# Batch 3 of a fused attention and bilinear kernel: block sums on GpSimd, multiplications on VectorE, x sums earlier, unused products spread over Sinkhorn's rounds

## The chip, the cores and the metric

The kernel runs on one core of a Trainium2 chip. The metric is the device time of one execution in microseconds (us). Three runs of the kernel before took 234.43, 234.69 and 235.43 us; the median is 234.69 us. In the rows, PE is TensorE, PEld its weight loads, DVE VectorE, ACT ScalarE, POOL GpSimd and SP SyncE, which issues DMAs.

## The reference

Four batches of eight heads, 768 positions, head width 64. An 8x8 matrix per head is made nearly doubly stochastic by five rounds of Sinkhorn, it mixes the eight blocks of k and v, and each block of q attends to its mixed block. The result, 3072 rows of 512, goes through a bilinear feed-forward layer.

```
P = sort_net
for _ in range(5):
    P = exp(P - max(P));  P = P / sum(P, axis=-1);  P = P / sum(P, axis=-2)
k_sorted, v_sorted = P applied to the 8 blocks of k and v
attn = softmax(q_block @ k_sorted_block.T / 8)
x = (attn @ v_sorted_block), reshaped to 3072 x 512
out = ((x @ w_a) * (x @ w_b)) @ w_out        # 512 -> 1536 -> 512
```

## The kernel before

**Tiling.** The four batches follow each other. A batch has 768 rows, so x transposed (`xT`) is four tiles of 128 x 768 and the hidden layer (`hT`) twelve of them. In the feed-forward layer, a = x w_a and b = x w_b are made in pieces of 128 hidden units by 384 rows (four products of 128x128 with 384 columns each, line 372), ScalarE copies a from PSUM to SBUF, and VectorE multiplies it with b, which it reads from PSUM (line 404). While TensorE does the layer of one batch, `interleave` slips the next batch's attention units between the steps. The order of instructions on every engine is the order in which the program writes them.

**Block products with fewer multiplications.** The output product h w_out is done by `ffn_out_pair` in three units of seven block products (42 products on TensorE each) in place of eight. It needs sums of blocks of h: `h_sums(b, m, nm)` (line 460) makes, for the pair of hidden tiles m and m + 6, three instructions: `hs[0]` and `hs[1]` in one (768 elements per partition), `hs[2]` (384), and one that overwrites two blocks of h in place (768). All stand at line 475 and run on VectorE; with nm = 2 one instruction serves two pairs. They wait in the list `sums_due` and are let out by `some_sums` between other work, or all at once by `sums_for` ahead of the first output unit. That unit reads, in order: h as it is (two block products), `hs[1]` (`add1`), `hs[0]` (`add3`), `hs[2]` (`add2`), then the two overwritten blocks.

**Batch 3.** The last batch has no attention beside it, and its a is made in the same way from sums of blocks of x and of w_a. `x_sum(3, n)`, n = 0 to 4, makes the sums of x on VectorE (line 578); in the kernel before they run in the last two steps of batch 2, 0 and 1 after the third of the four parts of the last output unit, and 2, 3 and 4 after the fourth. Then `ab_four(b, m)`, for m = 0 to 5, handles one pair of hidden tiles with 30 products of 384 columns:

```
a_product(acc0); a_product(acc1); a_product(pf1)     # y = acc0 + acc1 + pf1
b(1,0); a_product(acc0); b(0,1) after a_product(acc1)  # middle blocks h(1,0), h(0,1)
a_product(acc0); a_product(acc1); b(0,0); b(1,1)     # corners: a = y - acc
```

The order on TensorE is acc0, acc1, pf1 (two products each), b(1,0) (four), acc0, acc1 (two each), b(0,1) (four), acc0, acc1 (two each), b(0,0), b(1,1) (four each). The two `acc` are PSUM tiles that take three block products each in turn, so TensorE may go on adding only when the earlier content was read. In the kernel before, ScalarE copies both acc to SBUF (lines 622, 624), GpSimd adds them to y (line 625), and VectorE adds pf1 (line 628). For the middle blocks ScalarE copies b and a to SBUF (lines 613, 618) and GpSimd multiplies (lines 632, 636). VectorE makes both corners (line 642) and multiplies them with b from PSUM (line 645). The h sums go to VectorE's list after m = 1, 3, 4 and 5, for the pairs 0 and 1, 2 and 3, 4, and 5.

**The start.** Sinkhorn's chain of small instructions on VectorE and ScalarE takes five rounds. Beside it TensorE runs products of zeros whose result nobody reads (`keep_busy`, line 181), and transposes q of batch 0 (`first_q`, line 202) when its DMA has landed. `pace(t, n)` is one such product that reads t, the row or column sums of a round, and so waits for them, followed by n more.

Of the kernel before, what the change touches and what calls it, by code (L numbers as in the profile page):

```python
# [9 lines left out]
FP32 = mybir.dt.float32  # L10
# [13 lines left out]
def kernel(  # L24
# [154 lines left out]
    def keep_busy(ps, n, cols=512):  # L179
        for _ in range(n):  # L180
            nc.tensor.matmul(ps[:, 0:cols], lhsT=warm[:, 0:P], rhs=warm[:, 0:cols],  # L181
                             start=True, stop=True)
# [15 lines left out]
    def first_q(hp):  # L198
        q_ps = psF.tile([P, NCH, P], BF16, tag="F", name="q_ps")
        for c in range(NCH):  # L200
            for e in range(2):
                nc.tensor.matmul(q_ps[e * D:(e + 1) * D, c, :],  # L202
                                 lhsT=q_first[:, 2 * hp + e, c * D:(c + 1) * D],
                                 rhs=ident, is_transpose=True)
        st["q_ps", hp] = q_ps
# [177 lines left out]
    def some_sums(n):  # L383
        for _ in range(min(n, len(sums_due))):
            sums_due.pop(0)[1]()
# [71 lines left out]
    def h_part(b, r, c, m):  # L457
        return hTs[b][:, c * KH + m, r * HW:(r + 1) * HW]

    def h_sums(b, m, nm):  # L460
        n0, n = (P, HW - P) if b == 0 else (0, HW)
        if b not in sums:
            sums[b] = ffp.tile([P, KH, 3, HW], BF16, tag="hs", name="hs")
        hT, hs = hTs[b], sums[b]

        def h(r, c, step):
            return _ap(hT, (c * KH + m) * S + r * HW + n0,
                       [[KO * S, P], [S, nm]] + [[step, 2]] * (step is not None) + [[1, n]])

        def s(i, k):  # L470
            return _ap(hs, (m * 3 + i) * HW + n0,
                       [[KH * 3 * HW, P], [3 * HW, nm]] + [[HW, k]] * (k > 1) + [[1, n]])

        turn = KH * S - HW
        return [("h", lambda to=to, x=x, y=y, op=op: nc.vector.tensor_tensor(  # L475
                    out=to, in0=x, in1=y, op=op))
                for to, x, y, op in (
                    (s(0, 2), h(0, 0, 0), h(0, 1, HW), ALU.add),
                    (s(2, 1), h(1, 0, None), h(1, 1, None), ALU.add),
                    (h(1, 0, turn), h(0, 0, KH * S + HW), h(1, 0, turn), ALU.subtract))]  # L480
# [72 lines left out]
    C11, C12, C21, C22 = (w_a_sb[:, r * 2:(r + 1) * 2, c * DFF // 2:(c + 1) * DFF // 2]  # L553
                          for r in range(2) for c in range(2))
    a_sums, x_sums = {}, {}
    spare = {}

    def a_sum(n, kc):
        x, y = (C11, C12, C21, C21, C11)[n], (C22, C22, C11, C22, C12)[n]
# [31 lines left out]

    def ab_four(b, m):
        hT = hT_of(b)
        if m < 2:
            spare[m] = ld.tile([P, 2, HW], FP32, tag="kv", name="two_a")
        s2 = spare[m % 2]
        acc = [psA.tile([P, 2, 512], FP32, tag="A", name="acc")[:, 0, 0:HW] for _ in range(2)]
        y = ld.tile([P, HW], FP32, tag="q2", name="y_a")

        def a_tile():  # L600
            return ffp.tile([P, HW], BF16, tag="a_sb", name="a_sb", bufs=4)

        def b_of(c, t):
            pf = psF.tile([P, 512], FP32, tag="F", name="pf")
            ab_mms(pf, w_b_sb, b, m + c * KH, t, range(KA))
            return pf[:, 0:HW]

        def h(c, t):
            return hT[:, m + c * KH, t * HW:(t + 1) * HW]

        def kept_b(c, t):
            b_sb = ld.tile([P, HW], FP32, tag="q2", name="b_sb")
            nc.scalar.copy(out=b_sb, in_=b_of(c, t))
            return b_sb

        def middle(n):
            a_sb = a_tile()
            nc.scalar.copy(out=a_sb, in_=acc[n])
            return a_sb

        a_product(acc[0], (b, 0, 0), a_sums[1], m)
        nc.scalar.copy(out=s2[:, 0], in_=acc[0])
        a_product(acc[1], (b, 1, 1), a_sums[2], m)
        nc.scalar.copy(out=s2[:, 1], in_=acc[1])  # L624
        nc.gpsimd.tensor_tensor(out=y, in0=s2[:, 0], in1=s2[:, 1], op=ALU.add)  # L625
        pf = psF.tile([P, 512], FP32, tag="F", name="pf1")[:, 0:HW]
        a_product(pf, 0, a_sums[0], m)
        nc.vector.tensor_tensor(out=y, in0=pf, in1=y, op=ALU.add)
        b_sb = kept_b(1, 0)
        a_product(acc[0], 1, C22, m, False)  # L630
        a_sb = middle(0)
        nc.gpsimd.tensor_tensor(out=h(1, 0), in0=a_sb, in1=b_sb, op=ALU.mult)
        a_product(acc[1], 2, C11, m, False)
        a_sb = middle(1)
        b_sb = kept_b(0, 1)
        nc.gpsimd.tensor_tensor(out=h(0, 1), in0=a_sb, in1=b_sb, op=ALU.mult)
        some_sums(1)
        corners = []
        for n in range(2):
            a_product(acc[n], 3 + n, a_sums[3 + n], m, False)  # L640
            a_sb = a_tile()
            nc.vector.tensor_tensor(out=a_sb, in0=y, in1=acc[n], op=ALU.subtract)
            corners.append(a_sb)
        for n in range(2):
            nc.vector.tensor_mul(out=h(n, n), in0=corners[n], in1=b_of(n, n))  # L645
            some_sums(1)
        if m in (1, 3, 4, 5):
            sums_due[:0] = h_sums(b, *((m - 1, 2) if m < 4 else (m, 1)))

# [54 lines left out]
    with tc.manual_schedule(engines={ET.PE, ET.Pool, ET.SP, ET.Activation, ET.DVE}):  # L706
        if True:
# [14 lines left out]
                copy(eng, p_rep[:, hf * NR:(hf + 1) * NR],  # L722
                     _ap(p_fin, hf * NR, [[NB * NB, BH], [1, NR], [0, CG // 2]]))

            keep_busy(heat[:, 0], 46, P)
            for hp in range(HP):
                first_q(hp)
                if hp % 2:
                    keep_busy(heat[:, 0], 34 if hp == 1 else 2, P)
            for it in range(5):  # L730
                rsum, csum = chain[0][it], chain[1][it]
                nc.scalar.activation(out=p_nat, in_=p_nat, func=AF.Exp)
                if it == 2:
                    with nc.allow_low_precision("sum of one one and zeros"):
                        nc.vector.reduce_sum(
                            out=mask, in_=_ap(ident, 0, [[P, P], [1, CG], [CG, NB]]),
                            axis=AX.X)
                nc.vector.reduce_sum(out=rsum, in_=p_nat, axis=AX.X)
                nc.vector.reciprocal(out=rsum, in_=rsum)
                if it == 4:  # L740
                    pace(rsum, 10)
                nc.vector.tensor_mul(out=p_nat, in0=p_nat,
                                     in1=_ap(rsum, 0, [[NB, BH], [1, NB], [0, NB]]))
                nc.vector.reduce_sum(out=csum, in_=p_nat.transpose([0, 2, 1]), axis=AX.X)
                nc.vector.reciprocal(out=csum, in_=csum)
                if it == 4:
                    pace(csum, 6)
                if it < 4:
                    nc.vector.tensor_mul(out=p_nat, in0=p_nat,
                                         in1=_ap(csum, 0, [[NB, BH], [0, NB], [1, NB]]))  # L750
                else:
                    nc.vector.tensor_mul(
                        out=p_fin.bitcast(BF16).rearrange("h (i j u) -> h i j u", i=NB, j=NB),
                        in0=_ap(p_nat, 0, [[NB * NB, BH], [NB, NB], [1, NB], [0, 2]]),
                        in1=_ap(csum, 0, [[NB, BH], [0, NB], [1, NB], [0, 2]]))
                if it == 3:
                    first_q_out(0, "act")
            first_q_out(1, "act")
            first_q_out(2, "act")
            replicate("dve", 0)  # L760
# [104 lines left out]
        for b in range(1, B):  # L865
            ab = {}

            def ab_begun(m, t, b=b, ab=ab):
                if b == 1 and m == t == 0:
                    for key in ((0, w_a_sb), (0, w_b_sb)):  # L870
                        pf = psF.tile([P, 512], FP32, tag="F", name="pf")
                        ab.setdefault(key[0], []).append(pf)
                        ab_mms(pf, key[1], b, 0, key[0], range(KA - 1))
                return ab.get(t, ()) if m == 0 else ()

            steps = [lambda m=m, t=t, b=b: ffn_ab(b, m, t, ab_begun(m, t))
                     for m in halves for t in range(2)]
            if b == B - 1:
                steps = [lambda m=m, b=b: ab_four(b, m) for m in range(KH)]
            steps += outs(b)  # L880
            if b == 2:
                steps[1] = after(steps[1], lambda: sums_due.extend(
                    a_sum(n, kc) for n in (2, 3, 0, 1, 4) for kc in range(2)))
                steps[-2] = after(steps[-2], lambda: (x_sum(3, 0), x_sum(3, 1)))
                steps[-1] = after(steps[-1], lambda: (x_sum(3, 2), x_sum(3, 3), x_sum(3, 4)))
            interleave(steps, units_full(b + 1) if b + 1 < B else [],
                       (1, 4, 8, 10, 13, 15, 17, 20, 21, 24, 25, 28))

# [29 lines left out]
```

## Time and profile before

| what | us |
|---|---|
| median of three runs (lowest to highest) | 234.69 (234.43 to 235.43) |
| the profiled execution, its own time | 233.79 |
| its span, first to last instruction | 232.0 |
| around the span (233.79 - 232.0) | 1.79 |
| busy: TensorE / VectorE / ScalarE / GpSimd | 225.8 / 158.4 / 120.9 / 87.7 |
| batch 3, products for a and b begin | 183.23 |
| batch 3, first output product | 214.12 |
| TensorE begins the last twelve products | 227.38 |
| granted TensorE clock, mean | 0.999 |

Times in rows are from the start of the span. A row of a timeline gives the start, the time from the first instruction's start to the last one's end, the engine, the line, the operation with its tiles and the count, and in brackets for how long the engine had idled and what released it. Rows of one engine overlap a little, since an instruction begins while the one before it drains: the distance between starts is what an instruction costs in a row of equals, and its duration what a follower waits.

### The profile page before, as it was taken

Reading aid. Unit: us, or ns where it says so; the run is one execution under the profiler, and the core shown is the slowest. Engines: PE = TensorE matmul, PEld = TensorE weight load, DVE = VectorE, ACT = ScalarE, POOL = GpSimd, SP = SyncE. Lnnn points to the kernel's source line nnn. Section 1 sums busy time; section 2 is a strip of 40 time slices with the busy share of each in tenths; the row PEclk is TensorE's granted clock in tenths of the full one; section 3 lists DMA queues with packets and bytes.
Section 4 is the critical chain, followed back from the end, with each engine's and each line's share of the span. In section 5 each row is a group of like instructions: output and inputs, shape, how many; then the busy total and the mean of one; then the engine's idle time right before and its main releaser. Section 6 shows DMA issues by size and latency. Waiting matters only on the chain.

```text
span 232.0 us, 5823 instructions
## 1 busy us (share of the span) xinstructions
PE 225.8 (97%) x2281; PEld 158.9 (68%) x2283; DVE 158.4 (68%) x352; ACT 120.9 (52%) x260; POOL 87.7 (38%) x116
## 2 busy tenths in 40 slices
PE   7999999999999999999999999999999989999994
PEld 7876766766549865666689865666698745555783
DVE  7776777446999334758886347778785675979732
ACT  3575854687633375655552375656543445544231
POOL 8779839840041555237622010000000156766000
PEclk9999999999999999999999999999999999999999
DMA  5999999999759999998999454224025300000042
GB/s 71 201 201 199 206 204 199 196 196 157 133 86 213 144 201 170 165 186 110 132 179 209 158 127 79 42 41 82 12 47 155 132 34 0 1 0 3 2 168 104
DMA packets 54859, 28.70 MB, mean 124 GB/s; under 512 B 33712, under 2 KB 51888, under 8 KB 54832
## 3 DMA queue, kind: packets, MB, share of 16 engines
q0 software_dynamic: 18832, 14.16, 44.8%
q1 hardware_dynamic: 35856, 14.04, 31.7%
q8 instruction: 18, 0.29, 0.5%
q10 hardware_dynamic: 144, 0.13, 0.2%
q14 instruction: 9, 0.07, 0.1%
HBM read 28.32 MB, written 6.29 MB: 149 GB/s over the span
## 4 chain that ended last, share of the span: by engine, by line
PE 86%; DVE 7%; issue 2%; DMA 2%; ACT 1%; POOL 0%; POOLq 0%; DVEq 0%
PE pf L372 44%; PE po L484 21%; PE mix L312 3%; PE o_ps L278 3%; PE acc L588 3%; DMA first<-in_q_dram 2%; PE sc L333 2%; PE heat L181 1%; DVE x_sum L578 1%; DVE hT L475 1%; PE mixh L224 1%; PE sc L237 1%; DVE hs L475 1%; PE xt_ps L269 1%; PE q_ps L202 1%
## 5 line engine op out<-in xcount | busy, mean ns | idle before, releaser
L372 PE MATMUL pf<-xT,w_b_sb 128*128 128x384 bf16 x384 | 77.9, 326 | 0.0
L404 DVE TENSOR_TENSOR hT<-a_sb,pf 128x384 bf16<-128x384 bf16 x72 | 39.7, 552 | 38.1 <-ACT a_sb L403 22.9
L372 PE MATMUL pf<-xT,w_a_sb 128*128 128x384 bf16 x280 | 57.5, 326 | 0.0
L372 PEld LDWEIGHTS <-w_b_sb 128*128 128x128 bf16 x384 | 37.5, 98 | 24.9
L403 ACT CAST a_sb<-pf 128x384 bf16<-128x384 f32 x70 | 34.0, 486 | 33.7 <-PE pf L372 28.7
L372 PEld LDWEIGHTS <-w_a_sb 128*128 128x128 bf16 x288 | 25.9, 98 | 14.3
L484 PE MATMUL po<-w_sum,hT 128*128 128x256 bf16 x264 | 31.9, 273 | 0.3 <-DVE hT L645 0.3
L625 POOL TENSOR_TENSOR y_a<-two_a 128x384 f32<-128x384 f32 x6 | 6.0, 1005 | 58.5 <-ACT two_a L624 58.5
L484 PEld LDWEIGHTS <-hT 128*128 128x128 bf16 x264 | 25.4, 98 | 3.9 <-DVE hT L645 0.7
L175 ACT CAST kv<-mix 128x384 bf16<-128x384 f32 x48 | 19.5, 493 | 4.7 <-PE mix L312 4.6
L338 ACT ACTIVATE eT<-sc 96x768 bf16<-96x768 f32 x24 | 18.1, 802 | 6.0 <-PE sc L333 6.0
L484 PEld LDWEIGHTS <-hs 128*128 128x128 bf16 x198 | 19.1, 98 | 2.5 <-DVE hs L475 0.4
L475 DVE TENSOR_TENSOR hs<-hT 128x768 bf16<-128x768 bf16 (+5 forms) x32 | 20.4, 652 | 0.4
L505 DVE TENSOR_TENSOR o<-y,po 128x256 f32<-128x256 f32 x22 | 9.2, 420 | 11.9 <-PE po L484 11.9
L498 ACT COPY s<-po 128x256 f32<-128x256 f32 x22 | 8.0, 374 | 17.8 <-PE po L484 17.8
L284 DVE TENSOR_TENSOR xp<-o_ps,rec 96x512 bf16<-96x512 f32 x24 | 16.5, 687 | 0.8
L484 PE MATMUL po<-w_out_sb,hs 128*128 128x256 bf16 x132 | 16.4, 273 | 0.0
L111 POOL COPY kvc<-kv 128x768 uint32<-128x768 uint32 x16 | 13.3, 843 | 7.5 <-PE mix L312 7.2
L498 ACT COPY o<-po 128x256 f32<-128x256 f32 x22 | 8.2, 372 | 15.0 <-PE po L484 15.0
L299 POOL COPY qc<-q 128x384 uint32<-128x384 uint32 x12 | 6.4, 535 | 23.3 <-DMA q<-in_q_dram 18.3
L100 POOL DMA_DIRECT2D kv<-in_k_dram x16 | 11.6, 724 | 3.0 <-PE o_ps L278 2.1
L475 DVE TENSOR_TENSOR hT<-hT 128x1536 bf16<-128x1536 bf16 (+3 forms) x16 | 12.6, 786 | 0.1
(99 smaller groups left out, 303.1 us busy)
## 6 DMA issues: line engine op xcount, KB each, us to landing
out_dram<-o SPq DMA_DIRECT2D x17, 256.0 KB, 2.4
kv<-in_k_dram POOLq DMA_DIRECT2D x16, 192.0 KB, 7.6
kv<-in_v_dram POOLq DMA_DIRECT2D x16, 192.0 KB, 8.0
q<-in_q_dram POOLq DMA_DIRECT2D x12, 192.0 KB, 8.4
w_out_sb<-in_moe_w_out_dram POOLq DMA_DIRECT2D x3, 512.0 KB, 12.4
out_dram<-o SPq DMA_DIRECT2D x9, 128.0 KB, 6.7
w_a_sb<-in_moe_w_a_dram POOLq DMA_DIRECT2D x2, 512.0 KB, 11.0
w_b_sb<-in_moe_w_b_dram POOLq DMA_DIRECT2D x2, 512.0 KB, 12.6
```

The source lines that it names most:

```text
L100: nc.gpsimd.dma_start(out=to, in_=_ap(t, base, [[W, P], [S * D, 2], [1, W]]))
L111: nc.gpsimd.tensor_copy(out=to.bitcast(U32).rearrange("p c n d -> p n c d"), in_=loaded[g][0].bitcast(U32).rearrange("p n (c d) -> p n c d ...
L175: nc.scalar.copy(out=out, in_=in_)
L284: nc.vector.tensor_tensor(out=_ap(xp, i0 * 2 * D, [[nxp * 2 * D, BLK], [D, 2], [2 * D, NBH], [1, D]]), in0=_ap(o_ps, 1, [[1024, BLK], [511 ...
L338: nc.scalar.activation(out=eT[:, hf, :, 0:HB], in_=sc[0:BLK, :, 0:HB], func=AF.Exp, scale=float(scale))
L372: nc.tensor.matmul(pf[:, 0:HW], lhsT=w_sb[:, kc, m * P:(m + 1) * P], rhs=x_cols(b, kc, t), start=(kc == 0), stop=(kc == KA - 1))
L403: nc.scalar.copy(out=a_sb, in_=pf[:, 0:HW])
L404: nc.vector.tensor_mul(out=hT[:, m, t * HW:(t + 1) * HW], in0=a_sb, in1=ab[1][:, 0:HW])
L475: return [("h", lambda to=to, x=x, y=y, op=op: nc.vector.tensor_tensor(out=to, in0=x, in1=y, op=op)) for to, x, y, op in ((s(0, 2), h(0, 0 ...
L484: nc.tensor.matmul(to, lhsT=lhs(m)[:, u * P:(u + 1) * P], rhs=rhs[:, m], start=start and m == 0, stop=(m == KH - 1), skip_group_check=not ...
L498: nc.scalar.copy(out=to, in_=v["ps"][n])
L505: nc.vector.tensor_tensor(out=to, in0=v["y"], in1=v["ps"][n], op=ALU.subtract)
```

## The change

Four things, three of them in batch 3:

- `h_sums` takes the engine as an argument. After m = 0, 1, 2 and 3 the three sums of that pair are written to GpSimd at once (nm = 1). The sums of pairs 4 and 5 are put into the list together after m = 5 (nm = 2) and run on VectorE ahead of the first output unit's second part. `some_sums` is no longer called in `ab_four`.
- y: ScalarE copies acc0 only, straight into y; VectorE adds acc1 from PSUM, then pf1. The tile pair `two_a` is gone.
- The middle blocks are multiplied by VectorE, with b read from PSUM. ScalarE's two copies of b and GpSimd's two multiplications are gone.
- The x sums 0 and 1 run one step earlier (after the second part of batch 2's last output unit), 2 and 3 after the third part, and x sum 4 in `ab_four` of m = 0, behind the two additions to y.

At the start, the 46 unused products ahead of q's first transposes become 36 and two groups of 1 + 8 tied to the row and column sums of round 1; the 34 between the two halves of q become 14, and 1 + 8 and 1 + 4 tied to round 3; the 2 behind them go, and round 4 has 1 + 8 and 1 + 6 in place of 1 + 10 and 1 + 6. The second half of q's transposes comes after the products tied to round 3.

```
-    def h_sums(b, m, nm):
+    def h_sums(b, m, nm, eng=nc.vector):
...
     a_product(acc[0], (b, 0, 0), a_sums[1], m)
-    nc.scalar.copy(out=s2[:, 0], in_=acc[0])
+    y = ld.tile([P, HW], FP32, tag="q2", name="y_a")
+    nc.scalar.copy(out=y, in_=acc[0])
     a_product(acc[1], (b, 1, 1), a_sums[2], m)
-    nc.scalar.copy(out=s2[:, 1], in_=acc[1])
-    nc.gpsimd.tensor_tensor(out=y, in0=s2[:, 0], in1=s2[:, 1], op=ALU.add)
+    nc.vector.tensor_tensor(out=y, in0=acc[1], in1=y, op=ALU.add)
...
     nc.vector.tensor_tensor(out=y, in0=pf, in1=y, op=ALU.add)
-    b_sb = kept_b(1, 0)
+    if m == 0:
+        x_sum(b, 4)
+    pf = b_of(1, 0)
     a_product(acc[0], 1, C22, m, False)
-    a_sb = middle(0)
-    nc.gpsimd.tensor_tensor(out=h(1, 0), in0=a_sb, in1=b_sb, op=ALU.mult)
+    nc.vector.tensor_mul(out=h(1, 0), in0=middle(0), in1=pf)
     a_product(acc[1], 2, C11, m, False)
     a_sb = middle(1)
-    b_sb = kept_b(0, 1)
-    nc.gpsimd.tensor_tensor(out=h(0, 1), in0=a_sb, in1=b_sb, op=ALU.mult)
-    some_sums(1)
+    nc.vector.tensor_mul(out=h(0, 1), in0=a_sb, in1=b_of(0, 1))
...
         nc.vector.tensor_mul(out=h(n, n), in0=corners[n], in1=b_of(n, n))
-        some_sums(1)
-    if m in (1, 3, 4, 5):
-        sums_due[:0] = h_sums(b, *((m - 1, 2) if m < 4 else (m, 1)))
+    if m < KH - 2:
+        for _, run in h_sums(b, m, 1, nc.gpsimd):
+            run()
+    elif m == KH - 1:
+        sums_due[:0] = h_sums(b, m - 1, 2)
...
-    keep_busy(heat[:, 0], 46, P)
-    for hp in range(HP):
-        first_q(hp)
-        if hp % 2:
-            keep_busy(heat[:, 0], 34 if hp == 1 else 2, P)
...
+    keep_busy(heat[:, 0], 36, P)
+    round_of(0)
+    round_of(1, 8, 8)
+    first_q(0)
+    first_q(1)
+    keep_busy(heat[:, 0], 14, P)
+    round_of(2)
+    round_of(3, 8, 4)
+    first_q_out(0, "act")
+    first_q(2)
+    first_q(3)
+    round_of(4, 8, 6)
...
-    steps[-2] = after(steps[-2], lambda: (x_sum(3, 0), x_sum(3, 1)))
-    steps[-1] = after(steps[-1], lambda: (x_sum(3, 2), x_sum(3, 3), x_sum(3, 4)))
+    for n, of in ((-3, (0, 1)), (-2, (2, 3))):
+        steps[n] = after(steps[n], lambda of=of: [x_sum(3, i) for i in of])
```

`round_of(it, n_rows, n_cols)` is one round of Sinkhorn as before, with `pace(rsum, n_rows)` and `pace(csum, n_cols)` where the numbers are not zero.

More of the change, by code (lines that the diff above doesn't have):

```diff
@@ L474, in h_sums @@
         turn = KH * S - HW
-        return [("h", lambda to=to, x=x, y=y, op=op: nc.vector.tensor_tensor(
+        return [("h", lambda to=to, x=x, y=y, op=op: eng.tensor_tensor(
                     out=to, in0=x, in1=y, op=op))
@@ L555 @@
     a_sums, x_sums = {}, {}
-    spare = {}
     def a_sum(n, kc):
@@ L593, in ab_four @@
         hT = hT_of(b)
-        if m < 2:
-            spare[m] = ld.tile([P, 2, HW], FP32, tag="kv", name="two_a")
-        s2 = spare[m % 2]
         acc = [psA.tile([P, 2, 512], FP32, tag="A", name="acc")[:, 0, 0:HW] for _ in range(2)]
-        y = ld.tile([P, HW], FP32, tag="q2", name="y_a")
         def a_tile():
@@ L609, in h @@
             return hT[:, m + c * KH, t * HW:(t + 1) * HW]
[L611 to L614, printed above, removed]
         def middle(n):
@@ L723, in replicate, with round_of @@
                      _ap(p_fin, hf * NR, [[NB * NB, BH], [1, NR], [0, CG // 2]]))
-            keep_busy(heat[:, 0], 46, P)
-            for hp in range(HP):
-                first_q(hp)
-                if hp % 2:
-                    keep_busy(heat[:, 0], 34 if hp == 1 else 2, P)
-            for it in range(5):
+            def round_of(it, n_rows=0, n_cols=0):
                 rsum, csum = chain[0][it], chain[1][it]
@@ L739 @@
                 nc.vector.reciprocal(out=rsum, in_=rsum)
-                if it == 4:
-                    pace(rsum, 10)
+                if n_rows:
+                    pace(rsum, n_rows)
                 nc.vector.tensor_mul(out=p_nat, in0=p_nat,
@@ L745 @@
                 nc.vector.reciprocal(out=csum, in_=csum)
-                if it == 4:
-                    pace(csum, 6)
+                if n_cols:
+                    pace(csum, n_cols)
                 if it < 4:
@@ L755 @@
                         in1=_ap(csum, 0, [[NB, BH], [0, NB], [1, NB], [0, 2]]))
-                if it == 3:
-                    first_q_out(0, "act")
+            keep_busy(heat[:, 0], 36, P)
[10 more added lines that the diff above has]
+            round_of(4, 8, 6)
             first_q_out(1, "act")
```

## The prediction

> **What bounds the kernel now.** I read the busy times first, then the chain of waits in order of time, then busy time by stage, then the timelines of the two stages that the change touches. TensorE is busy for 225.8 of 232.0 us and makes up 86% of the chain, so only time in which it stands still, or work of its own, can be saved. The change removes no product outside the start. Busy time by stage (columns: stretch, length, then busy time and count of PE, PEld, DVE, ACT and POOL, clock, DMA) hides the holes, because a product's row is 326 ns while products follow every 162 ns:
>
> ```profile
> 183.23:214.12 30.89, 30.14 (x183) 17.43 (x181) 25.15 (x41) 15.67 (x36) 19.19 (x18) 1.00 0.05 19
> 214.12:216.90 2.78, 2.39 (x20) 1.52 (x18) 2.78 (x8) 0.74 (x2) 0.31 (x1) 1.00 0.00 0
> ```
>
> So I count products. In TensorE's timeline, pair m = 1 of batch 3 runs without a hole:
>
> ```profile
> 189.09 0.81 PE L588 MATMUL acc<-xT,a_sum 128*128 128x384 bf16 x4
> ...
> 190.71 0.81 PE L588 MATMUL acc<-x_sum,w_a_sb 128*128 128x384 bf16 x4
> ...
> 193.96 0.81 PE L588 MATMUL acc<-xT,a_sum 128*128 128x384 bf16 x4
> ```
>
> A pair takes 193.96 - 189.09 = 4.87 us for its 30 products, so six take 29.22 us; the stage takes 30.89. **1.67 us are holes.** The chain shows the first and the second, larger group of them (start, length, what):
>
> ```profile
> 183.39 0.65 PE acc L588 x4
> 184.13 0.33 DVE o L505
> 184.46 2.94 DVE x_sum L578 x3
> 187.45 0.50 PE acc L588 x2
> ...
> 214.97 0.34 DVE hs L475
> 215.32 0.47 DVE hT L645
> 215.84 0.33 issue
> 216.18 0.56 DVE hs L475
> 216.78 12.09 PE po L484 x109
> ```
>
> The reader is to see that the x sums carry the chain at 184 to 187 (TensorE's own timeline shows products until 186.59 and again from 187.45: 0.86 us lost), and that at the end VectorE's sums are late. The three output units have 126 products, and 109 are left at 216.78: the 18th, the last of `add1`, starts there. From 214.12, 17 products of 0.109 us (12 from 180.61 to 181.92) end at 215.97, so **0.81 us are lost in this tail**. The rest of the 1.67 lies ahead of m = 3 and m = 5 (each third of a microsecond, after VectorE spent 1.6 us on one sum). Upper bound of the gain in batch 3: 1.67 + 0.81 = 2.48 us.
>
> **Part 1, x sums.** Sums 0 and 1 now follow the addition to y at 181.09 (0.42), so they run from about 181.55 at 0.47 a piece (two took 1.02 at 183.11), done at 182.6, ahead of the corner at 182.77 that stands behind them. What they wait for, the last transpose into xT, was issued at 175.88 and takes 2.8 us: landed by 178.7. Sums 2 and 3 take the slots of 0 and 1 (183.11 to 184.13), and the second corner starts at 184.05 as now. Three sums in a row took 1.0 each, because GpSimd worked beside them; now it does nothing then. Sum 4 sits behind y's additions, ends near 186.1 and is wanted at T + 3.25 = 186.48 (T is a pair's start). SP's and POOL's queues are not passed. Gain: 0.86 us.
>
> **Part 2, y and middle blocks.** I rebuild one pair from the rows of m = 1. ScalarE's copy of acc0 starts at T + 0.56 and lasts 0.48: 1.04. A follower on another engine started 0.15 later (GpSimd at 190.66 after ScalarE's 190.51). VectorE's addition then runs 1.19 to 1.75 (0.56, the row of line 628). TensorE wants acc1 again at T + 1.95 (the third product of the group at 190.71): **0.20 us of slack**, where formerly a copy had to be done. Second addition: 1.85 to 2.41 (0.10 between dependents, as from 187.86 to 187.96). Middle blocks: a copied by about 2.7 and 3.1, b(0,1) there at about 3.17, multiplications at 2.8 and 3.25. Corners from 3.72 and 4.19; h(0,0) at 4.66; h(1,1) waits for b and ends at T + 5.62, as now (193.51 + 1.20 = 194.71). Corner 1 has read acc1 by 4.75, needed at 5.20. VectorE has eight instructions at 0.47 = 3.8 us of 4.87; the list's 1.6 us pieces are gone from its way. The holes ahead of m = 3 and m = 5 go with them. Gain: 1.67 - 0.86 = 0.81 us, if the slack holds. What was ScalarE's and GpSimd's work had cost nothing by itself.
>
> **Part 3, h sums on GpSimd.** The trace has no bf16 sum on GpSimd. Nearest rows (mean ns last):
>
> ```profile
> L167 POOL TENSOR_TENSOR s_all<-mask,p_col 128x1024 bf16<-128x1024 bf16 x3 | 6.1, 2019 | 0.0
> ...
> L167 POOL TENSOR_TENSOR s_all<-mask,p_col 128x512 bf16<-128x512 bf16 x1 | 1.1, 1105 | 0.0
> ```
>
> From these: 0.19 us + 1.79 ns an element, so 1.56 for 768 and 0.88 for 384; a pair is 1.56 + 0.88 + 1.56 = 4.0 us. The other rows are the multiplications of 384 with an fp32 operand: 0.92 undisturbed makes 5 x 0.92 = 4.6, and the longest, 1.59, makes 7.95. Below 3.5 nothing points. I take 4.0, the row with the same type. Pair 3 begins at 183.23 + 3 x 4.87 + 5.72 = 203.56 and ends at 207.6 (208.2 with 4.6). The first output unit wants it from 213.9 on: hidden, with five us to spare.
>
> Do the two engines hold each other up? From VectorE's timeline:
>
> ```profile
> 196.93 1.58 DVE L475 TENSOR_TENSOR hs<-hT 128x1536 bf16<-128x1536 bf16 x1
> 198.44 1.01 DVE L642 TENSOR_TENSOR a_sb<-y_a,acc 128x384 bf16<-128x384 f32 x2
> ```
>
> and from GpSimd's timeline:
>
> ```profile
> 197.70 1.59 POOL L636 TENSOR_TENSOR hT<-a_sb,b_sb 128x384 bf16<-128x384 bf16 x1
> ```
>
> The same sum of 1536 took 0.96 at 157.47, where GpSimd was idle; beside GpSimd both stretch. The corners (one operand in PSUM) kept 1.01 a pair beside GpSimd, and GpSimd kept 0.92 beside them at 192.82. In the new order, VectorE's only instructions with both operands in SBUF are sum 4 (GpSimd not yet started) and the sums of pairs 4 and 5 (GpSimd done). So nothing stretches. The Trainium skill, "Perfetto Trace Analysis", section "Optimizing Scalar/DVE Operations", speaks against such a change: it warns that moving work between VectorE and GpSimd might not help, as they share a read port. "SBUF — State Buffer", section "Who interferes with whom", narrows that to VectorE instructions with two inputs in SBUF, which is what the rows above show; by the first page the gain of this part would be put at nothing, by the second it stays.
>
> **Part 4, the tail.** Pair 5 starts at 183.23 + 5 x 4.87 = 207.58 and TensorE reaches the first output product at 212.45. h(1,1) ends at 207.58 + 5.62 = 213.20, wanted by the 12th product at 213.65. VectorE then makes `hs` of pairs 4 and 5: 213.30 + 0.96 = 214.26, and the fifth product of `add1` can start at 214.32; it would want to at 212.45 + 16 x 0.109 = 214.19. So the 18th starts at 214.43 in place of 216.78. `hs[2]` follows at 214.75 (wanted about 215.5), the overwritten blocks at about 215.8 (wanted for pair 4 at 216.15), y's additions by 216.7, and the corner at 216.8 uses them. **The sum: 216.78 - 214.43 = 2.35 us**; everything behind is unchanged (109 products, then the last store).
>
> **Part 5, the start.** The Sinkhorn chain sets it, and TensorE must only be ready at 11.6. Rows:
>
> ```profile
> 1.27 5.09 PE L181 MATMUL heat<-warm 128*128 128x128 bf16 x46 [1.27 <-DVE warm L86]
> 6.40 0.81 PE L202 MATMUL q_ps<-ident,first 128*64 128x128 bf16 x22
> ```
>
> 46 products at 0.107 us are at the slow rate; the 34 behind took 2.00, 0.059 each. New: 36 end near 5.1, the row sums of round 1 are ready at 4.8, nine products end at 6.1, nine more by 6.7 to 7.0; q's first half 0.3 to 0.6 later, done before ScalarE fetches it at 7.77. Fourteen products end by 8.7; round 3's sums come at 8.3 and 9.1, so q's second half runs 9.5 to 10.3, round 4's products follow, and the last seven end at 11.4, before the products at 11.61. Cost: nothing, hidden by the chain; without that cover each 0.1 us is 0.1 us. TensorE has no hole over 0.4 us in it, no longer than those of 12 to 20 us, where the rate stayed high. Bounds: 0 to +1.6 us, if q's 48 transposes ran at half rate (48 x 0.033 us more) and were not covered; I take 0, since the present start has the same margin.
>
> **Rivals.** (1) *The slack in part 2 fails.* Copy and addition in series, 0.2 us late in all six pairs: 1.2 us back, and 2.35 - 1.2 leaves a gain of 1.15. Against it, each duration is from a row; for it, 0.20 us is the narrowest place. (2) *Slower: GpSimd's sums are late.* At 7.95 us a pair (4.1 ns an element, the stretched row) four of them end at 188.95 + 31.8 = 220.75, while the overwritten block of pair 3 is wanted at 212.45 + 33 x 0.109 = 216.05: 4.7 us of waiting, less the gain 2.35, is 2.35 slower. It decides from (216.05 + 2.35 - 188.95) / 4 = 7.4 us a pair. Against it: nothing left beside GpSimd has two operands in SBUF. (3) *Nothing gained:* the start loses what batch 3 gains, with TensorE at the slow rate into the mixes: +1.6, net gain 0.7 or less. For it: tied products leave small holes that the present start lacks.
>
> **Numbers.** The profiled execution took 233.79 us (span 232.0, 1.79 around it): 233.79 - 2.35 = 231.44. The runs shown have the median 234.69, 0.90 above it; the measure is a median of runs, so I forecast 234.69 - 2.35 = 232.3. Chances: forecast 0.70, rival (1) 0.12 (233.5), rival (3) 0.08 (234), rival (2) 0.10 (237). Range: from 231.3 (the whole 2.48, and runs that fall like the profiled one) to 234.0, which takes in (1) and part of (3). About 0.5% (1.2 us) is what a measurement can tell from no change: faster 0.77 (forecast and part of (1)), same 0.13, slower 0.10.
>
> **What would show it.** Right: no hole on TensorE between batch 3's first product and its first output product (29.2 us between them), the 18th output product some 31.2 us after that first product, GpSimd's sums of a pair near 4.0 us and done before the tail, corners still 1.01 a pair. Wrong: a hole ahead of the second use of acc1 in each pair (rival 1), GpSimd as releaser of TensorE in the output unit (rival 2), a later `to_columns` product than 11.6 (rival 3).

## The result and the profile after

The changed kernel took 231.99 us, median of four runs (231.69 to 232.68), beside 235.06 us for the kernel before (234.43 to 236.32): a ratio of 0.987, 95% interval 0.982 to 0.992. On another chip, with more runs (e5 below), it was 231.64 (231.48 to 233.90) against 233.88: 0.991, 0.988 to 0.994. The two agree; the second, -2.2 us, is the tighter one. The forecast was 232.3, a gain of 2.35. Ratios, here and below, leave out the few runs that show a lower granted clock (one of e1's six, among others); the medians do not.

The profiled execution shows where it came from. Busy time by stage in the changed kernel (stretch, length, busy time and count of PE, PEld, DVE, ACT, POOL, clock, DMA), from batch 3's first product to the first output product, and on past the 18th, to 215.83:

```profile
184.42:213.68 29.26, 29.26 (x182) 17.60 (x180) 25.20 (x51) 8.04 (x18) 16.63 (x12) 1.00 0.05 20
213.68:215.83 2.15, 2.15 (x22) 1.78 (x20) 2.12 (x4) 0.75 (x2) 0.00 (x0) 1.00 0.00 0
```

The stage takes 29.26 us, six times 4.87 within 0.04, and TensorE is never idle in it. The end of the chain of waits is now a single block; where 109 output products stood behind VectorE's sums, all 126 follow the layer's last product directly:

```profile
212.55 1.30 PE pf L372 x8
213.85 13.84 PE po L484 x126
227.71 0.42 DVE o L505
```

From batch 3's first product to the first product of the third block (`add3`), which I call **the stretch** below, it is 215.72 - 184.42 = 31.30 us, against 216.90 - 183.23 = 33.67 before: **2.37 us**, where 2.35 was worked out. GpSimd's timeline has the new sums, one pair as an example (the first row is two instructions):

```profile
199.89 2.51 POOL L475 TENSOR_TENSOR hs<-hT 128x768 bf16<-128x768 bf16 x2 [0.64 <-DVE hT L634]
202.48 1.65 POOL L475 TENSOR_TENSOR hT<-hT 128x768 bf16<-128x768 bf16 x1
```

A pair takes 4.2 us (4.0 was reckoned) and GpSimd then waits 0.64 for the next. But the start went against the prediction. Batch 3 began at 184.42, not at 183.23: the profiled execution is only 1.1 us shorter than that of before (232.68 against 233.79), and it is the slowest of its four runs. TensorE's timeline at the start of the changed kernel:

```profile
8.92 0.21 PE L705 MATMUL heat<-warm,rsum 32*8 32x128 bf16 x1
...
10.09 0.86 PE L202 MATMUL q_ps<-ident,first 128*64 128x128 bf16 x24
...
12.17 0.26 PE L765 MATMUL pc_ps<-ident,p_rep 32*128 32x32 bf16 x4
...
15.45 0.38 PE L224 MATMUL mixh<-s_all,kv 128*64 128x64 bf16 x12 [0.21 <-DMA kv<-in_k_dram]
```

Two things are late. The first product that reads p_rep comes at 12.17 (11.61 before), though VectorE had p_rep's half ready at 11.55: TensorE was still working through its unused products. And the load of k for the third of the four head pairs landed late (15.45). The experiments separate the two.

### The profile page after: what moved, and what is told of

The parts are those of the page before. It is cut to its first block, busy times and chain, and to the rows that moved or that the text cites. A ratio compares the mean times of both kernels' runs of the same rounds, so it can differ in the third digit from the quotient of the medians.

```text
span 230.8 us, 5798 instructions
## 1 busy us (share of the span) xinstructions
PE 225.5 (98%) x2279; PEld 159.0 (69%) x2281; DVE 159.7 (69%) x361; ACT 113.3 (49%) x242; POOL 85.8 (37%) x110
## 4 chain that ended last, share of the span: by engine, by line
PE 89%; DMA 4%; DVE 3%; POOL 2%; issue 1%; ACT 0%; POOLq 0%; DVEq 0%
PE pf L372 47%; PE po L484 22%; PE acc L587 5%; DMA kv<-in_k_dram 4%; PE mix L312 3%; PE o_ps L278 3%; PE sc L333 2%; POOL kv L100 1%; PE pf L587 1%; PE sc L237 1%; PE xt_ps L269 1%; POOL first L93 1%; DVE w_sum L453 1%; DVE xp L284 1%; PE mixh L224 1%; PE vs_ps L254 1%
## 5 line engine op out<-in xcount | busy, mean ns | idle before, releaser
L475 POOL TENSOR_TENSOR hs<-hT 128x768 bf16<-128x768 bf16 (+1 forms) x8 | 10.0, 1277 | 56.4 <-PE acc L587 54.5
L475 DVE TENSOR_TENSOR hs<-hT 128x768 bf16<-128x768 bf16 (+5 forms) x26 | 15.5, 614 | 0.4
L299 POOL COPY qc<-q 128x384 uint32<-128x384 uint32 x12 | 7.1, 589 | 21.1 <-DMA q<-in_q_dram 15.7
L100 POOL DMA_DIRECT2D kv<-in_k_dram x16 | 11.6, 725 | 3.0 <-PE o_ps L278 2.1
L100 POOL DMA_DIRECT2D kv<-in_v_dram x16 | 11.5, 722 | 3.0 <-DMA first<-in_q_dram 1.5
```

The source lines that it names most:

```text
L100: nc.gpsimd.dma_start(out=to, in_=_ap(t, base, [[W, P], [S * D, 2], [1, W]]))
L475: return [("h", lambda to=to, x=x, y=y, op=op: eng.tensor_tensor(out=to, in0=x, in1=y, op=op)) for to, x, y, op in ((s(0, 2), h(0, 0, 0), ...
```

## The experiments

Each time is a median and each ratio stands against the kernel before, run on the same chip; "stretch" is as above, and "p_rep product" is the start of the first product that reads p_rep. The last three have one run each.

| run | us | ratio (95% interval) | stretch | p_rep product |
|---|---|---|---|---|
| before | | 1 | 33.67 | 11.61 |
| changed, first result | 231.99 | 0.987 (0.982 to 0.992) | 31.30 | 12.17 |
| e1 batch 3 only | 231.93 | 0.991 (0.987 to 0.994) | 31.30 | 11.70 |
| e2 start only | 234.30 | 1.001 (0.999 to 1.003) | 33.67 | 12.26 |
| e3 sums back on VectorE | 235.53 | 1.006 (1.004 to 1.009) | 34.88 | 12.31 |
| e4 lighter start | 231.59 | 0.990 (0.986 to 0.994) | 31.31 | 11.62 |
| e5 changed again | 231.64 | 0.991 (0.988 to 0.994) | 31.30 | 12.00 |
| e6 no unused products | 236.53 | 1.012 (1.008 to 1.016) | 31.30 | 11.51 |
| e7 x sums only | 233.15 | 0.998 (0.996 to 1.000) | 32.68 | 11.58 |
| e8 VectorE sums beside GpSimd's | 232.66 | 0.994 (0.991 to 0.996) | 31.87 | 11.85 |
| e9 GpSimd sums twice | 233.20 | 0.995 (0.992 to 0.997) | 31.74 | 11.79 |
| e10 GpSimd sums three times | 243.81 | | 42.05 | 12.00 |
| e11 y late | 235.41 | | 35.08 | 11.83 |
| e12 sums on GpSimd, nothing else | 247.80 | | 45.94 | 11.65 |

### Which part of the change: e1 and e2

My theory was that batch 3 gives the whole gain and the start nothing; the rivals were that the start costs half a microsecond, or gains what the first medians showed beyond 2.35. e1 is the changed kernel with the old start, e2 the kernel before with the new one:

```
e1:  -            keep_busy(heat[:, 0], 36, P)
     ...          (and the rounds with tied products)
     +            keep_busy(heat[:, 0], 46, P)
     +            for hp in range(HP):
     +                first_q(hp)
     ...
e2:  the same lines the other way round, in the kernel before
```

> All of the change in batch 3, with the start of the kernel before (46 and 34 unused products, q's halves as before). Theory A: batch 3 gives 2.35 us and the start edits nothing; what the profiled start of the changed kernel lost (batch 3 begins 1.2 us later) is a landing of loads that differs from run to run. Then this run is at a ratio of 0.990 to the kernel before (-2.35 of 235), within 0.2% of the changed kernel's mean. Theory B: the new start costs the 0.56 us by which its first product that reads p_rep is late (12.17 against 11.61): then this run is 0.5 to 0.6 us faster than the changed kernel, 0.984 to 0.985. Theory C: the new start gains the 0.7 us by which the medians fell further than 2.35: then 0.990, and slower than the changed kernel by 0.7. In every case the stretch from batch 3's first product to the 18th output product is 31.3 us, as in the changed kernel.

> The kernel before with only the start of the changed kernel (36, 1+8, 1+8, 14, 1+8, 1+4, 1+8, 1+6 unused products and q's second half behind round 3). Theory A: 1.000 within 0.002. Theory B: slower by 0.5 to 0.6 us, 1.0025. Theory C: faster by 0.7 us, 0.997. The holes of batch 3 stay: 33.6 us from its first product to the 18th output product.

Measured: 0.991 and 1.001, with stretches of 31.30 and 33.67. The gain is batch 3's, to the tenth of a microsecond in the traces. The new start neither gains nor loses anything that can be told from no change, although e2's trace has the p_rep product at 12.26 again. The times cannot say more: e2's interval (0.999 to 1.003) rules out the gain of 0.7 us (0.997), but holds the 1.0025 of a start that costs half a microsecond as well as 1.000, and e1 beside e5, 0.991 both with intervals 0.006 to 0.007 wide, is no sharper.

### The start: e4, e5 and e6

```
e4:  keep_busy 28, 8 in place of 36, 14; round_of(1, 6, 4), (3, 4, 2), (4, 4, 4)
e5:  no edit, the changed kernel
e6:  -  keep_busy(heat[:, 0], 36, P), keep_busy(heat[:, 0], 14, P)
     +  round_of(1), round_of(3), round_of(4) without tied products
```

> The changed kernel with fewer unused products at the start: 28 in place of 36, 1+6 and 1+4 in round 1, 8 in place of 14, 1+4 and 1+2 in round 3, 1+4 and 1+4 in round 4, so that TensorE has no backlog when p_rep is there. Theory B (backlog costs): the first product that reads p_rep at 11.6 in place of 12.2, 0.5 us faster than the changed kernel. Theory A (the landing of k and v sets the start): the mixes of pairs 1 to 3 still wait for their loads, same time within 0.2 us. If the slow rate of the clock lasts longer with fewer products, q's transposes take 1.6 in place of 0.8 us a half and the run is 0.5 to 1.5 us slower.

> The changed kernel itself, on one chip with the two runs behind it, so that the starts can be set side by side. If its new start costs the 0.6 us that the traces of two kernels with that start show (first product that reads p_rep at 12.26 and 12.31, against 11.70 and 11.62), its lowest time is 0.2 to 0.6 us above that of the kernel with fewer unused products (231.44 against a kernel before of 233.74 on another chip) and its ratio about 0.990 to 0.992. If the profiled execution was an accident of its loads and the start costs nothing, its ratio is 0.988 to 0.990. First product that reads p_rep: 12.2 to 12.3 again, whatever the loads do; second half of q's load landed at 8.5, not 9.7.

> The changed kernel with none of the unused products at the start (36, 14 and all tied groups gone; q's halves stay where they are). If they do nothing but fill TensorE's queue, the first product that reads p_rep comes at 11.6 and the run is as fast as the one with fewer of them, 0.990. If they are what brings the clock to its full rate, q's first transposes and what follows run at half rate for some 5 us from 6.4 on (46 unused products ran at 0.107 us from 1.27 to 6.2): the products between 11.6 and the first layer's, 3 to 4 us of work if the slow rate lasts until then, take up to twice as long, and the run is 1 to 3 us slower, 0.995 to 1.003.

With fewer products the backlog is gone from the trace: e4's p_rep product stands at 11.62, and TensorE has gaps in which it waits for the sums. Yet the time is the same: 231.59 (lowest 231.44) against 231.64 (lowest 231.48) for e5, and 0.990 against 0.991 with wide overlap. e5's own profiled execution, with the p_rep product at 12.00, took 231.97, 0.3 above its median. With this start the p_rep product stood anywhere from 11.79 to 12.31 in eight traces, with the old start and e4's between 11.58 and 11.70 in five. In a profiled execution that lateness goes through whole: batch 3 begins 171.60 to 171.68 us behind the first p_rep product in the traces of the kernel before, e1 to e5 and e9 to e11. So the backlog is real in the profiled executions and costs them up to 0.7 us, but the timed ones do not show its price, and their intervals would hide half a microsecond. How large the backlog gets follows how long TensorE's slow rate lasts at the start: the trace's first clock record (a note of the granted clock with its start and length), at the full clock, begins at 4.38 in e9, 6.41 in e5, 7.05 in e2 and 7.16 in e3, and their p_rep products stand at 11.79, 12.00, 12.26 and 12.31. Which of these a timed run resembles stays open, since it has no trace. The late load belongs to that one execution: the load of q's second half, issued at the same time, released GpSimd's next load at 9.72 there, and at 8.49 in e5. It put batch 3 another 0.64 us behind (172.25 in place of 171.61). Three other traces lose time at another place that no edit touches: at 81 to 82 us TensorE waits 1.10 us (e7), 0.34 (e8) and 1.54 (e12) for a DMA into xT. This is why the stretch, and not the time of one execution, is the measure of batch 3.

e6 shows what the unused products are for. TensorE's timeline in it, a batch of transposes, a later product of the first layer, and one after 26 us:

```profile
6.31 1.49 PE L202 MATMUL q_ps<-ident,first 128*64 128x128 bf16 x24 [6.31 <-DMA first<-in_q_dram]
...
24.23 0.84 PE L372 MATMUL pf<-xT,w_b_sb 128*128 128x384 bf16 x2
...
26.08 0.49 PE L372 MATMUL pf<-xT,w_b_sb 128*128 128x384 bf16 x2
```

Transposes take 1.49 in place of 0.86, and two products of the layer 0.84 until about 26 us, then 0.49. Without the unused products TensorE runs at the slow rate until then, and batch 3 begins 4.6 us later than in e5 (188.25 against 183.68). The columns of busy time for that span deceive:

```profile
16.00:20.00 4.00, 4.00 (x67) 2.87 (x61) 1.63 (x4) 2.24 (x4) 4.00 (x6) 1.00 1.45 196
```

TensorE is 100% busy, and the granted clock reads 1.00, yet 67 products run here and 91 in the same stretch of e5. The column reads 1.00 wherever the trace holds no clock record, and e6's first record, at the full clock, begins at 25.87, just where the durations fall (in the kernel before it begins at 6.26). Ahead of the first record, the durations alone show the rate. The Trainium skill, "TensorE: Matmul & The Clock Gate", "What's actually happening", gives some 3.4 us of sustained work until the full rate. In these traces the first record begins 3.0 (e4) to 5.9 us (e3) behind the first unused product at 1.27. In e6 the short products kept TensorE's busy column full from 12 us on, and still the full rate came only at 25.87. So e4 and e9 (3.1) are near the page's figure, and e6 is not; why it came so late, no run shows.

### What the parts of batch 3 are worth: e7, e3 and e12

```
e7 (kernel before):  x_sum(3, 0), (3, 1) in steps[-3];  (3, 2), (3, 3), (3, 4) in steps[-2]
e3 (changed kernel): -  h_sums(b, m, 1, nc.gpsimd) for m < KH - 2
                     +  sums_due[:0] = h_sums(...) after m = 1, 3, 4, 5, some_sums(1) as before
e12 (kernel before): +  h_sums(b, m, 1, nc.gpsimd) for m < KH - 2, pairs 4 and 5 on VectorE
```

> The kernel before with only the x sums moved: 0 and 1 one step earlier, 2, 3 and 4 in the slots where 0 and 1 stood. The prediction's part 1 says that the hole between 186.59 and 187.45 goes: 0.86 us, 0.9963. Rival: pair 0 then waits for something else (GpSimd's addition to y, then its multiplications, still stand in line), and less than 0.4 us comes out, 0.998 or more. The holes ahead of pairs 3 and 5 and in the tail stay.

> The changed kernel with the h sums back on VectorE, let out one by one between its other work as before (after m = 1, 3, 4, 5); GpSimd has no work left in batch 3, so nothing stretches (a sum of 1536 at 0.96, not 1.58). My theory: VectorE's eight instructions at 0.47 and 1.1 us of sums a pair make 4.9 of 4.87 us, and a sum of 0.9 stands ahead of corners that TensorE waits for: small holes at the pairs with sums and in the tail, together 0.4 to 1.2 us slower than the changed kernel, 0.992 to 0.995. Rival: it was the stretching by GpSimd alone that made the holes, and the move of the sums to GpSimd gives nothing: as fast as the changed kernel within 0.2 us.

> The kernel before with the h sums of pairs 0 to 3 written to GpSimd after their pair, and those of 4 and 5 together on VectorE, and nothing else: GpSimd keeps y's addition and the two middle multiplications. It then has 1.0 + 0.92 + 0.92 + 4.2 = 7.0 us a pair for 4.87 us of products, and y's addition of the next pair stands behind 4.2 us of sums: pairs 1 to 4 begin about 2.2 us late each, 8 to 9 us slower than the kernel before, 241 to 243. If GpSimd's order did not matter and only VectorE's relief counts, it gains 1 us or more.

**e7.** The stretch shrank by 33.67 - 32.68 = 0.99. The hole at the x sums is gone, pair 1 begins 4.88 after pair 0 (189.33 and 184.45), the other holes stand. By the trace, part 1 was right. The times are weaker: the median fell by 0.73, and the ratio, 0.998 (0.996 to 1.000), fits the rival's 0.998 or more as well as the 0.9963 expected.

**e3** is the most telling run. Without GpSimd in batch 3 nothing stretches (a sum of 1536 takes 0.95), and still it is 1.2 us worse in the stretch than the kernel before, and 3.6 worse than the changed one; I had expected 0.4 to 1.2. VectorE's timeline, then TensorE's:

```profile
200.56 0.95 DVE L475 TENSOR_TENSOR hT<-hT 128x1536 bf16<-128x1536 bf16 x1
201.42 0.56 DVE L615 TENSOR_TENSOR y_a<-acc,y_a 128x384 f32<-128x384 f32 x1
```

```profile
200.59 0.49 PE L587 MATMUL acc<-x_sum,w_a_sb 128*128 128x384 bf16 x2
202.03 0.48 PE L587 MATMUL acc<-x_sum,w_a_sb 128*128 128x384 bf16 x2 [0.95 <-DVE y_a L615]
```

A sum of two pairs stands ahead of y's first addition, which has to read acc1 before TensorE may use it again: TensorE stands still for 0.95 us, twice. Besides, pairs 3 and 5 still begin 0.3 us late, where a corner stands behind a sum (the corner at 198.23 behind the sum at 197.36), and the first output unit loses some 0.5 again. This is rival 1 of the prediction, set off by the queue in front of the addition. The rival theory, that the stretching by GpSimd made all the holes, falls: nothing stretches here, and the holes ahead of pairs 3 and 5 are still there.

**e12** is the other half: the sums go, GpSimd keeps its three other instructions. It lost 13.6 us, 12.3 of them in the stretch, more than the 8 to 9 expected. Its waits, in total, times and longest:

```profile
DVE y_a L628 <- POOL y_a L625: 22.6, 5, 5.3
...
PE acc L588 <- DVE a_sb L642: 9.1, 4, 2.8
```

Pairs 2 to 4 take 7.95 us each, pair 1 takes 7.43. I had added up GpSimd's own 7.0; but its sums wait for VectorE's products, which wait for y, which stands behind the sums on GpSimd: a ring, whose VectorE part (1.04 us of GpSimd waiting a pair) I left out. After two of TensorE's waits its slow rate also came back: the granted clock was 0.50 from 199.64 to 203.06 and from 223.54 to 226.95, and the last pair took 6.69 in place of 4.87. So neither move gains by itself, in the orders tried (a sum placed behind y's first addition was not): the middle blocks and y must leave GpSimd to make room for the sums, and the sums must leave VectorE to make room for the middle blocks and y.

### Do the two engines hold each other up: e8, e9 and e10

```
e8:   +  nc.vector.tensor_tensor(out=idle, in0=x_sums[0], in1=x_sums[1], op=ALU.add)  behind y, m >= 1
e9:   -  for _, run in h_sums(b, m, 1, nc.gpsimd):
      +  for _, run in h_sums(b, m, 1, nc.gpsimd)[:2] * 2 + h_sums(b, m, 1, nc.gpsimd)[2:]:
e10:  the same with * 3
```

> The changed kernel with one more VectorE sum per pair m = 1 to 5, 768 elements bf16 with both operands in SBUF (x sums 0 and 1, result unused), behind the two additions to y, in VectorE's idle time and while GpSimd works on the h sums of pairs 0 to 3 (pair 5 has no GpSimd work beside it). If instructions with both operands in SBUF hold each other up on the two engines: 0.55 us alone (m = 5), 1 us or more beside GpSimd, or GpSimd's sums grow from 4.2 us a pair; the middle blocks come late, and holes of 0.3 us or more open in the pairs 1 to 4, 1 to 2 us in all. If not: 0.55 us everywhere, and not over 0.2 us in all.

> The changed kernel with the first two of GpSimd's three sums of each pair (hs[0] and hs[1], hs[2]) written twice over; the third is not repeated, the result is the same. A pair then takes 2 x 2.51 + 1.65 + 0.1 = 6.8 us on GpSimd in place of 4.2, and four of them end at T0 + 5.71 + 27.1 = T0 + 32.8 (T0 is batch 3's first product), just when the third sum of pair 3 is wanted, T0 + 32.86. If that room is what hides GpSimd's work, nothing is lost, or 0.3 us at most: 31.3 to 31.6 from T0 to the third block product, 0.990 to 0.992. If GpSimd's work costs something while it runs (VectorE or TensorE held up), the loss grows with it: 60% more work, each pair later, over 0.5 us.

> The same with the first two sums three times: 3 x 2.51 + 1.65 + 0.1 = 9.3 us a pair, four of them end at T0 + 42.9, and the products that want the third sum of pair 3 at T0 + 32.86 wait for it: 10 us slower than the changed kernel, 241 to 242, with GpSimd as releaser of TensorE's weight loads in the first output unit, and still no hole in the six pairs. That is rival 2 of the prediction made to happen. If GpSimd held up the other engines while it runs, the pairs would have holes too.

**e8**, VectorE's timeline: the added sum of pair 4, with GpSimd at work, and the multiplication after it; then the sum of pair 5, without GpSimd:

```profile
206.27 1.08 DVE L624 TENSOR_TENSOR idle<-x_sum,x_sum 128x768 bf16<-128x768 bf16 x1
207.28 0.54 DVE L627 TENSOR_TENSOR hT<-a_sb,pf 128x384 bf16<-128x384 bf16 x1
...
211.19 0.55 DVE L624 TENSOR_TENSOR idle<-x_sum,x_sum 128x768 bf16<-128x768 bf16 x1
```

1.08 against 0.55, while the multiplication, with one operand in PSUM, keeps 0.54; GpSimd's first two sums grow from 2.51 to 2.82. The direction was right, the price was not: 0.57 us in the stretch instead of 1 to 2, since a pair has idle time that takes most of it up: pair 2 begins some 0.46 late, and each pair after it loses some 0.04. This agrees with the rule of the Trainium skill, "SBUF — State Buffer", "Who interferes with whom", that the prediction weighed.

**e9** missed. The six pairs have no hole, as expected, but the trace is 1.4 us longer in the first output unit (0.9 by the ratios). VectorE, GpSimd and TensorE there:

```profile
213.46 3.31 DVE L475 TENSOR_TENSOR hs<-hT 128x1536 bf16<-128x1536 bf16 x2
```

```profile
214.12 2.23 POOL L475 TENSOR_TENSOR hT<-hT 128x768 bf16<-128x768 bf16 x1
```

```profile
214.91 0.39 PE L484 MATMUL po<-w_sum,hs 128*128 128x256 bf16 x2 [0.34 <-DVE hs L475]
...
216.82 0.39 PE L484 MATMUL po<-w_out_sb,hs 128*128 128x256 bf16 x2 [0.42 <-DVE hs L475]
```

VectorE's sums of pairs 4 and 5 take 3.31 in place of 1.43, because GpSimd is still at work beside them, until 216.35. The room that hides GpSimd's sums does not end where TensorE wants them, but 2.8 us earlier, where VectorE begins its own (213.46 - 183.40 = 30.06 us into the batch). With 4 pairs from 5.7 us on, that is an estimate of 6.1 us a pair from which GpSimd's sums begin to cost something, where the prediction's figures give 6.8, (216.05 - 188.95) / 4. Its 7.4 is the pace at which the whole gain would be gone; e9, at 6.65 a pair, has already lost 1.4.

**e10**: 243.81, 12 us slower than the changed kernel, the six pairs still free of holes, and GpSimd as releaser:

```profile
225.05 0.82 PE L484 MATMUL po<-w_sum,hs 128*128 128x256 bf16 x3 [10.37 <-POOL hs L475]
225.66 2.72 PE L484 MATMUL po<-w_out_sb,hs 128*128 128x256 bf16 x12
```

That is rival 2 made to happen. The second row is a price that no expectation had: after 10.4 us of standing still, TensorE's next 12 products take 2.72 in place of 1.47. The granted clock was 0.50 from 217.96 to 228.20.

### The slack ahead of acc1: e11

```
e11:  +  for _ in range(2): nc.scalar.copy(out=idle, in_=acc[0])
         nc.scalar.copy(out=y, in_=acc[0])
```

> The changed kernel with two more copies of acc0 on ScalarE (384 elements, result unused) ahead of the copy into y: y's first addition comes 2 x 0.38 = 0.76 us later. With the slack that the trace of the changed kernel shows (addition ends at T + 1.60, wanted at T + 1.95, some 0.06 to pass it on: 0.29) a hole of 0.47 opens ahead of the second use of acc1 in each pair, 2.8 us in six. With the 0.20 on record: 0.56 a pair, 3.4 us. If the order has more room than that (rival 1 was no danger): under 1 us.

A pair takes 5.52 (188.90 to 194.42) in place of 4.87, so 0.65 us was lost in each, and 3.8 in the stretch; TensorE's row shows where, with ScalarE's late copy as releaser of acc0, and the group of four then taking 1.08 in place of 0.81:

```profile
190.90 1.08 PE L587 MATMUL acc<-x_sum,w_a_sb 128*128 128x384 bf16 x4 [0.21 <-ACT y_a L617]
```

The late copy delays both: acc0 by itself, and acc1 through VectorE's addition. How much was added is read from ScalarE's timeline and VectorE's in the same pair, and from VectorE's in pair 5 of the changed kernel:

```profile
189.48 0.99 ACT L616 CAST idle<-acc 128x384 bf16<-128x384 f32 x2 [2.50 <-PE acc L587]
190.37 0.48 ACT L617 COPY y_a<-acc 128x384 f32<-128x384 f32 x1
```

```profile
190.89 0.56 DVE L619 TENSOR_TENSOR y_a<-acc,y_a 128x384 f32<-128x384 f32 x1 [1.04 <-ACT y_a L617]
```

```profile
209.85 0.56 DVE L615 TENSOR_TENSOR y_a<-acc,y_a 128x384 f32<-128x384 f32 x1 [0.28 <-ACT y_a L613]
```

The two copies took 0.89 us, not the 0.76 expected, and the addition ends at T + 2.55 (T = 188.90) in place of T + 1.60 (T = 208.81), 0.95 later. Of that, 0.65 came through, so the order has 0.30 us of room there: what the trace of the changed kernel had suggested (0.29), and 0.1 more than the 0.20 on record.

## Why the prediction was right

**Part 1** (0.86 us): e7 shows 0.99 in its trace and 0.73 in its median. Right, and somewhat larger than reckoned: pair 0 of the kernel before took 189.09 - 183.23 = 5.86, 0.99 more than 4.87, so that of the 1.67 us of holes only 0.68 lay ahead of pairs 3 and 5 and not 0.81. The sum is the same.

**Part 2** (0.81 us, by the pairs 0.68, if 0.20 us of slack holds): the holes ahead of pairs 3 and 5 are gone and none opened. The rows were shorter than reckoned: in pair 5 the copy starts at T + 0.52 and y's first addition ends at 210.41 = T + 1.60, not 1.75. Only pair 1 came to the edge, by 0.02 us: its copy starts at T + 0.85, for a reason that the trace does not give. e11 shows that the slack is narrow, though 0.30 and not 0.20, e3 that rival 1 was the right thing to fear.

**Part 3**: 4.0 us a pair, measured 4.2; corners and their multiplications kept 1.01 to 1.04 a pair beside GpSimd. That GpSimd's sums and VectorE's hold each other up when both read two operands from SBUF is shown by e8 and e9; VectorE's instructions with an operand in PSUM kept their time.

**Part 4** (0.81 us less 0.13): TensorE lost 0.07 in `add1` (0.89 for six products against 0.82 in the other units). Right.

**Part 5** was the step that failed, without harm to the sum. "Fourteen products end by 8.7; [...] so q's second half runs 9.5 to 10.3" and the last seven "end at 11.4, before the products at 11.61" was reckoned with 0.55 us for a tied product and eight more. In the profile such a group takes 0.70 (8.92 to 9.62), since the tied product costs 0.15 and not 0.06, and at the slow rate 1.16 (5.22 to 6.38). Four groups and a second half of q in line made TensorE 0.56 us late: q's second half ran at 10.09 to 10.88. TensorE was the late one at 11.6, not the Sinkhorn chain. In that execution the 0.56 us went through to batch 3. The timed runs do not show them (e2, e4, e5) and are too scattered to exclude them, so the forecast of no cost stood, but not for the reason given: that part was luck.

**Rival 2's price** was mis-sized: the cost begins at about 6.1 us a pair (estimated from e9) and not at 6.8, since VectorE's last sums are held up before TensorE waits for GpSimd's.

**The median.** The first result's fall of 3.07 is 0.7 more than the traces explain. e1 and e5, with more runs, give 2.1 to 2.2; I take the surplus for scatter, which both intervals allow.

## What to carry to other kernels

When TensorE is the bound, count its products times their pitch in each stage and compare with the stage's length: the holes are the whole prize, and each has one releaser to remove. Before work is given to GpSimd, ask which instructions of VectorE will then run beside it with both operands in SBUF: those pay, the ones that read PSUM do not, and the room to hide GpSimd's work ends where the first of those begins. Work that moves between two engines may have to move in both directions at once (e3 and e12 each lose; together, with the x sums, which alone are worth 1.0 in the stretch, they gain 2.4 there), and what stands in an engine's queue ahead of the instruction that frees a PSUM tile costs its length less the slack there (0.65 of 0.95 us in e11). A clock column that reads 1.00 at the head of a span is no proof of the full rate: compare the durations of equal products.

## What the runs showed of the hardware

- TensorE ran at its slow rate until 25.87 us when nothing had kept it busy before its first real work (e6: two products of 384 columns took 0.84, then 0.49), although it was busy without a pause from 12 us on. With unused products from 1.27 on, the full rate came at 4.26 (e4) to 7.16 us (e3), by the first clock records.
- It fell back to the slow rate behind 10 us of standing still (e10: granted clock 0.50, 2.72 for 12 products that take 1.47), and in e12 behind two of its waits of 2.4 to 2.8 us (granted clock 0.50 for 3.4 us each).
- A sum of 768 bf16 elements on VectorE took 0.55 alone and 1.08 to 1.27 beside GpSimd's sums (e8); two sums, of 1536 and 768, took 1.43 together alone (changed kernel) and 3.31 beside GpSimd's (e9).
- GpSimd's bf16 sums took 1.64 for 768 elements and 0.87 for 384 (2.51 less 1.64): 2.1 to 2.3 ns an element.
